# Attention and two dense layers on one core: a third score buffer, one score a round, v loaded in eight halves, w_in decoded in fixed rounds

## The chip, the core and the metric

The program runs on one core of a Trainium2 chip. The metric is the device time of one execution in microseconds. The kernel before takes 887.46 us in the median of three runs (885.88 to 888.39). The profile was taken of a further execution of 892.93 us.

## The reference

There are three layers one after the other. The first is attention with batch 4, 12 heads, 448 positions and 64 features a head, in which two 12x12 matrices mix the heads, one before the softmax and one after it:

```
scores = q k^T / 8                              # b h i j
scores = einsum('bhij,hg->bgij', scores, w_pre)
attn   = softmax over j of scores
attn   = einsum('bhij,hg->bgij', attn, w_post)
x      = attn @ v                               # then (b, s, 768)
```

The second layer computes `h = gelu(x @ w_in)` with 1024 columns, splits it in `u` and `v`, normalises `v`, mixes its positions with a 448x448 matrix, and returns `x + (u * v_s) @ w_out`. The third rotates `x` by angles `x @ w_theta`, mixes positions with two 448x448 matrices, and adds `relu(u @ w_ch)`. Inputs are float32; the dense weights come as 64-bit words that the kernel decodes into a high and a low part.

## The kernel before, in words

Attention works on tiles `(b, t)`: in each of 4 batches the 448 queries are cut into tiles of 120, 120, 120 and 88 (`TILES`). A *round* is the unit of the loop at the end of `attention` (`for r in range(-LR, NR + 7)`). It handles a pair of blocks of ten queries by twelve heads, 120 partitions a block. A 120-query tile has 6 rounds, the 88-query tile has 4 rounds of pairs and one of a single block of eight queries. So a batch has 23 rounds, and there are `NR` = 92. Batch 1 begins at round 23, batch 2 at 46, batch 3 at 69.

For a tile, `scores(b, t, c)` runs six times, once for each pair of heads c: 8 matmuls q k^T into PSUM tile `psA` (one buffer of two banks), and one ScalarE copy into the tile's SBUF buffer `s` (pool `a_s`, L225). When all six are there, `relayout` (L236) sends the rows of a block through a DMA from `s` into a buffer `blk`, so that heads and queries lie on partitions; it is issued four rounds before the block is used (`LR`). There are six `blk` buffers, for three rounds. Two rounds before use (`LQ`) `premix` multiplies by w_pre into `psB` (L244), `rowmax` takes the maximum on VectorE (L250), and `expo` the exponential on ScalarE (L258). Then `recip` (GpSimd, L264), `recip2` (VectorE, L269) and `weigh` (GpSimd, L280) scale w_post by the reciprocal sums. In its own round `postmix` multiplies by those weights into `psC` (L302, three buffers, two a round). `at_hi` (ScalarE, L325) and `at_lo` (VectorE, L331) split the result in two float16 parts. When a tile is finished `attn_v` multiplies by v (L354), one c a round in the rounds behind it, and `out_x` and `store_x` write it to the scratch tensor xT.

Within a round each engine gets its instructions in the order of the loop body: relayout of round r+4, the list `early`, postmix, recip2 and weigh of the next round, `at_hi`, `at_lo`, the lists `front` and `mid`, premix to recip of round r+2, the second `at_lo`, then the lists `work` and `late`. Which step stands in which round and list is written out by the `put` calls. Every load and store goes through one queue, that of SyncE (SPq), in program order. A DMA in this queue that has to wait holds up those behind it.

The places that the change touches:

- *Score buffers.* `a_s` has two buffers. The scores of a tile begin in the round behind the one in which the last relayout of the tile two before it is issued, and that tile's buffer is the one they write. The function `units` spreads the six scores of a tile over the rounds of the tile before. As an 88-query tile has five rounds, one round in each batch gets two scores (rounds 14, 37 and 60).
- *v.* For batches 1 to 3, `load_v` loads v in four pieces (rounds 8, 7, 5 and 4 before z, with z the round before the batch), 128 partitions x 768 columns each (the last one on 64). `v_max` (L154) takes maxima two rounds later on VectorE, `v_turn` and `v_spread` carry them across partitions with two small matmuls into a tile `psV` from pool psA, and `v_mul` (GpSimd, L188), `v_hi` (VectorE, L193) and `v_lo` (GpSimd, L197) split v in two float16 parts, one c a round over six rounds.
- *Decoding of w_in.* 18 jobs (`extra`) decode 128x256 blocks: a load into `draw` in early of round W-2, ScalarE and VectorE steps in rounds W to W+2 (`words`, `value`, `high`, `low`), among them the ScalarE copy into `dh` in round W+1 (L602), and in early of round W+4 a store of `dh` to the scratch tensor win_d (L618). Pool `a_dec` has one buffer of each, so the copy of a job into `dh` waits until the store of the job before has landed. `JR0` and `JR1` place the jobs evenly: W = 8, 12, 16, 20, 25, 29, 33, 37, 42, 46, 50, 55, 59, 63, 67, 72, 76, 80.

At the end of attention the pools on the right side of SBUF are closed and the dense layers' tiles take their place; the loads of x and of the decoded w_in are issued from round 88 on (`tail`).

Of the kernel before, what the change touches and what calls it, by code (L numbers as in the profile page):

```python
# [6 lines left out]
F32 = mybir.dt.float32  # L7
# [5 lines left out]
ALU = mybir.AluOpType  # L13
AX = mybir.AxisListType
PSUM = bass.MemoryType.PSUM

B, H, S, D = 4, 12, 448, 64
NP = H // 2
# [9 lines left out]
LR, LQ = 4, 2  # L28
QO = 3
WARM = 8  # L30
JR0, JR1 = 8, 7
EXP_BITS = 0x7F800000


def attention(tc, nc, io, xT, B, extra, tail):
# [8 lines left out]
    NR = len(pairs)  # L44
    tiles = [(b, t) for b in range(B) for t in range(len(TILES))]
    nt = len(tiles)
    first, last = {}, {}
# [4 lines left out]
    with ExitStack() as es:  # L52
        early_es = ExitStack()

        def pool(name, bufs, **kw):
            return es.enter_context(tc.tile_pool(name=name, bufs=bufs, reuse_waits="tile", **kw))

        def pool_r(name, bufs, **kw):
            return early_es.enter_context(tc.tile_pool(name=name, bufs=bufs, side="right", reuse_waits="tile", **kw))

        s_p = pool_r("a_s", 2)
        k_p = pool_r("a_k", NP + 3)
        q_p = pool_r("a_q", 3)
        vr_p = pool_r("a_vr", 1)
# [1 line left out]
        psA = pool_r("psA", 1, space=PSUM)  # L66
# [9 lines left out]
        psC = pool("psC", 3, space=PSUM)  # L76
# [17 lines left out]
        ps = psC.tile([128, 512], F32, tag="psC", name="warm_ps")  # L94
# [36 lines left out]
        raws, kt, qt = {}, {}, {}  # L131
# [12 lines left out]
        vraw = vr_p.tile([128, 4, NP, 128], F32, name="vraw")  # L144
        nc.gpsimd.memset(vraw[:64, 3], 0.0)

        def load_v(b, j):
            p = slice(0 if j < 3 else 64, 128)
            nc.sync.dma_start(out=vraw[p, j], in_=io["vN"][b, 128 * j:min(128 * j + 128, S)].rearrange("p (c d) -> p c d", d=128))

        def v_max(b, j):
            if j == 0:
                raws["vmx", b] = sm_p.tile([128, 4, NP], F32, tag="vmx", name="vmx", bufs=1)
            nc.vector.tensor_reduce(out=raws["vmx", b][:, j], in_=vraw[:, j], axis=AX.X, op=ALU.max,  # L154
                                    apply_absolute_value=True)

        def v_join(b):
# [3 lines left out]

        def v_turn(b):

            ps = raws["vps", b] = psA.tile([128, 2, 512], F32, tag="psA", name="psV")[:, 0]
            nc.tensor.matmul(ps[:NP, :128], raws.pop(("vmx", b)), ident, start=True, stop=True)

        def v_top(b):
# [4 lines left out]

        def v_spread(b):

            ps = raws["vps", b] = psA.tile([128, 2, 512], F32, tag="psA", name="psV")[:, 0]
            nc.tensor.matmul(ps[:, :NP], ones, raws.pop(("dg", b)), start=True, stop=True)

        def v_scale(b):
# [191 lines left out]
        early, front, mid, work, late = {}, {}, {}, {}, {}  # L370

        def put(d, r, fn, *a):
            d.setdefault(r, []).append((fn, a))

        def units(T):
            lo, hi = first[tiles[T - 1]] - LR, first[tiles[T]] - LR - 1
            return [lo + (c * (hi - lo + 1)) // NP for c in range(NP)]

        for T in range(1, nt):
            b, t = tiles[T]  # L380
            u = units(T)
            for c in range(NP):
                put(front if u[c] not in u[:c] else work, u[c], scores, b, t, c)
            if T > 1:
                put(early, u[0] - QO, load_q, b, t)
            if t == 0:
                for c, r in enumerate(units(T - 1)):
                    put(early, r, load_k, b, c)
        for b in range(B):
            f = first[b, 0]  # L390
            z = f - 1 if b else 3
            for j, d in enumerate((8, 7, 5, 4) if b else (5, 4, 3, 2)):
                put(early, z - d, load_v, b, j)
                put(late, z - d + 2 if b else min(z - d + 2, z - 1), v_max, b, j)
            put(late, z - 1, v_join, b)
            put(work, z, v_turn, b)
            put(late, z, v_top, b)
            put(work, z + 1, v_spread, b)
            put(late, z + 1, v_scale, b)
            for c in range(NP):  # L400
                put(mid, z + 2 + c, v_mul, b, c)
                put(late, z + 2 + c, v_hi, b, c)
                put(mid, z + 3 + c, v_lo, b, c)
        for T in range(nt):
            b, t = tiles[T]
            for c in range(NP):
                if T == nt - 1:
                    r = last[b, t] + 1 + c // 3
                else:
                    r = last[b, t] + (min(2 + c, 6) if T == 0 else min(1 + c, 5 if t == 2 else 6))  # L410
# [2 lines left out]
                    put(late, r, out_x, b, t, c // 3)  # L413
                    put(early, r + (2 if T < nt - 1 else 1), store_x, b, t, c // 3)

        for j, fn in enumerate(extra):
            r = JR0 + (NR - JR0 - JR1) * j // len(extra)
            put(early, r - 2, fn[0], dec)
            words, value, high, low = fn[1:5]
            for i in range(2):  # L420
                put((mid, late)[i], r, words, dec, i)
                put((mid, late)[i], r + 1, high, dec, i)
            put(late, r, value, dec)
            put(late, r + 1, low, dec, 0)
            put(mid, r + 2, low, dec, 1)
            put(early, r + 4, fn[5], dec)
# [788 lines left out]
def build(tc, nc, io, out):  # L1215
    with tc.manual_schedule(), ExitStack() as top:
        dram = top.enter_context(tc.tile_pool(name="scratch", bufs=1, space=bass.MemoryType.DRAM))
        xT = dram.tile([DM, B * S], F32, name="xT")
        x2T = dram.tile([DM, B * S], F32, name="x2T")
        d = Dense(tc, nc, io, xT, x2T, out)  # L1220
        d.scratch(dram)
        right, left1, left2 = ExitStack(), ExitStack(), ExitStack()
        tail, win_es, last_u, end = moe1(d, left1, right)
        th_es = moe2(d, left2, win_es, last_u, left1)
        for i in range(4):
            tail.setdefault(-2 + 2 * i, []).append(d.step)
        jobs = d.decode_all(io["w_in"], HF, DFF, d.win_d)
        jobs += d.decode_all(io["w_in"], 0, HF, d.win_d, 128 * KE)
        attention(tc, nc, io, xT, B, jobs, tail)
        while d.at < len(d.units):  # L1230
            d.step()
        th_es.close()
        right.close()
        left2.close()
# [74 lines left out]
```

## Time and profile before

| what | value |
|---|---|
| median of three runs | 887.46 us |
| profiled execution | 892.93 us |
| its span, first to last instruction | 891.2 us |
| TensorE busy, share of the span | 854.0 us, 96% |
| VectorE, ScalarE, GpSimd busy | 74%, 60%, 28% |
| attention, to the first dense matmuls | to about 376 us |
| granted TensorE clock, mean | 0.992 |

The profile's busy times are means over the whole span. The attention rounds end at about 362 us; from 376 us on TensorE works on the dense layers almost without a gap. A table of stretches counts the matmuls of one line in each, and since a round of a pair has 64 postmix matmuls (L302), the count gives the number of rounds in the stretch.

### The profile page before, as it was taken

How to read it: one execution, taken by the hardware profiler on the slowest of the kernel's cores; microseconds unless marked ns; L12 is line 12 of the kernel's file. 1: busy time of each engine (PE TensorE's matmuls, PEld its weight loads, DVE VectorE, ACT ScalarE, POOL GpSimd, SP SyncE). 2: the span in 40 equal slices, each digit the busy share in tenths (PEclk: the TensorE clock that was granted, in tenths of full speed). 3: DMA queues.
4: the chain of work that ended last, by engine and by line, in shares of the span. 5: the costliest groups of instructions: out<-in, count | busy, mean ns of one | idle time of the engine just before them, and what ended most of it. 6: DMA issues, size and time to landing. Idle time of an engine off the chain costs nothing.

```text
span 891.2 us, 29399 instructions
## 1 busy us (share of the span) xinstructions
PE 854.0 (96%) x12008; PEld 673.9 (76%) x12008; DVE 660.7 (74%) x1471; ACT 535.3 (60%) x1202; POOL 253.9 (28%) x453
## 2 busy tenths in 40 slices
PE   8899999999998999799999999998999999999998
PEld 2456556565665566589898989898989999999997
DVE  3887888788888888579999998969886358338221
ACT  5888789878897887466665767427535136016010
POOL 0272254225422642000000000016607228406421
PEclk9999999999999999899999999999999999999999
DMA  6567656675676545873385857997620311300301
GB/s 203 193 210 220 212 176 213 207 230 175 217 229 201 186 168 141 270 239 98 111 280 172 279 182 234 294 348 248 212 92 29 114 34 39 114 22 7 105 20 63
DMA packets 116343, 151.15 MB, mean 170 GB/s; under 512 B 26224, under 2 KB 100208, under 8 KB 116208
## 3 DMA queue, kind: packets, MB, share of 16 engines
q1 hardware_dynamic: 116208, 149.26, 52.8%
q8 instruction: 95, 1.56, 0.8%
q14 instruction: 40, 0.33, 0.1%
HBM read 78.38 MB, written 32.31 MB: 124 GB/s over the span
## 4 chain that ended last, share of the span: by engine, by line
PE 67%; DVE 9%; DMA 8%; ACT 6%; POOL 5%; issue 4%; SPq 1%; ACTq 0%; POOLq 0%; DVEq 0%
PE ps L554 46%; PE psC L302 6%; PE psB L244 5%; PE psA L219 4%; PE psD L354 4%; ACT e L258 2%; POOL vl L197 2%; ACT s L225 2%; DVE nmx L250 1%; DMA win_d<-dh 1%; POOL vraw L188 1%; DMA blk<-s 1%; POOL wr L280 1%; DMA xres<-xT 1%; ACT ah L325 1%
## 5 line engine op out<-in xcount | busy, mean ns | idle before, releaser
L258 ACT ACTIVATE e<-psB,nmx 128x448 f32<-128x448 f32 x180 | 113.1, 637 | 32.8 <-DVE nmx L250 31.6
L331 DVE SCALAR_TENSOR_TENSOR al<-psC,ah 128x480 f16<-128x480 f32 x180 | 116.3, 647 | 9.7 <-ACT ah L325 8.8
L250 DVE TENSOR_REDUCE nmx<-psB 128x1 f32<-128x448 f32 x180 | 103.9, 618 | 16.2 <-PE psB L244 13.9
L302 PE MATMUL psC<-wr,e 64*64 64x60 f32 x5632 | 106.4, 222 | 4.3 <-issue 1.9
L550 POOL TENSOR_TENSOR x2s<-x,x2s 128x384 fp32r<-128x384 f32 x28 | 28.8, 1049 | 284.8 <-ACT x2s L547 284.8
L244 PE MATMUL psB<-blk,kpre 64*64 64x448 f32 x720 | 104.0, 546 | 4.8 <-ACT e L258 3.9
L302 PEld LDWEIGHTS psC<-wr,e 64*64 64x64 f32 x5632 | 93.7, 135 | 17.0 <-POOL wr L280 7.5
L554 PE MATMUL ps<-wtok,z 128*128 128x448 f32 x504 | 104.8, 368 | 0.0
L219 PE MATMUL psA<-k,q 64*64 64x448 f32 (+2 forms) x768 | 96.5, 551 | 7.8 <-ACT s L225 5.6
L554 PEld LDWEIGHTS ps<-wtok,z 128*128 128x128 f32 x504 | 94.6, 188 | 9.5
L354 PEld LDWEIGHTS <-vh 128*64 128x64 f16 x1536 | 57.5, 112 | 58.0 <-issue 57.8
L325 ACT ACTIVATE ah<-psC 128x480 f16<-128x480 f32 x180 | 93.7, 581 | 10.3 <-PE psC L302 10.2
L554 PE MATMUL ps<-wth,x2s 128*128 128x384 f32 x504 | 93.0, 338 | 3.2 <-POOL x2s L550 2.1
L225 ACT ACTIVATE s<-psA 124x896 f32<-124x896 f32 (+1 forms) x90 | 84.2, 936 | 12.3 <-PE psA L219 7.6
L554 PEld LDWEIGHTS ps<-wth,x2s 128*128 128x128 f32 x504 | 87.1, 188 | 4.9 <-POOL x2s L550 3.0
L554 PE MATMUL ps<-u,wch 128*128 128x448 f32 x432 | 89.9, 368 | 0.0
L554 PEld LDWEIGHTS ps<-u,wch 128*128 128x128 f32 x432 | 81.1, 188 | 8.1
L550 POOL TENSOR_TENSOR z<-zz,z 128x384 fp32r<-128x384 f32 x56 | 64.4, 1170 | 55.7 <-ACT z L547 55.6
L244 PEld LDWEIGHTS psB<-blk,kpre 64*64 64x64 f32 x720 | 37.6, 132 | 50.0 <-ACT e L258 23.8
L547 ACT ACTIVATE u<-xres 128x448 fp32r<-128x448 f32 x24 | 13.8, 577 | 99.1 <-DVE xres L1123 99.1
L264 POOL TENSOR_SCALAR rc<-sum 128x2 f32<-128x2 f32 (+1 forms) x92 | 22.4, 244 | 176.1 <-ACT e L258 175.0
L280 POOL TENSOR_SCALAR wr<-w,rc 128x60 f32<-128x60 f32 x180 | 54.5, 317 | 53.3 <-DVE rc L269 43.0
(129 smaller groups left out, 1614.5 us busy)
## 6 DMA issues: line engine op xcount, KB each, us to landing
blk<-s SPq DMA_DIRECT2D x176, 210.0 KB
draw<-in_w_in SPq DMA_DIRECT2D x24, 256.0 KB
k<-in_kvT SPq DMA_DIRECT2D x24, 224.0 KB
xraw<-xT SPq DMA_DIRECT2D x24, 224.0 KB
xres<-xT SPq DMA_DIRECT2D x24, 224.0 KB
x2T<-xres SPq DMA_DIRECT2D x24, 224.0 KB
xres<-x2T SPq DMA_DIRECT2D x24, 224.0 KB
out<-uu SPq DMA_DIRECT2D x24, 224.0 KB
```

The source lines that it names most:

```text
L219: nc.tensor.matmul(ps[e][r, :S], q[p, o + r.start:o + r.stop], k[p], start=True, stop=True)
L225: nc.scalar.activation(out=out, in_=pair[:m, :, :S], func=AF.Copy, scale=0.125)
L244: nc.tensor.matmul(ps[e][c:c + 64, :S], kpre[k, e], blk[k], start=True, stop=True)
L250: nc.vector.tensor_reduce(out=nmx[r][:, e:e + 1], in_=ps[:, :S], axis=AX.X, op=ALU.max, negate=True)
L258: nc.scalar.activation(out=x, in_=ps[:, :S], func=AF.Exp, bias=m[:, e:e + 1], accum_out=sm[:, e:e + 1])
L280: nc.gpsimd.tensor_scalar(out=w, in0=wts[n], scalar1=rc[:, e:e + 1], scalar2=0.0, op0=ALU.mult, op1=ALU.add)
L302: nc.tensor.matmul(pc[r][h][c:c + 64, jc, :, SQ * e:SQ * e + SQ], x[p, c:c + 64], wr[r][e][p], start=(e == 0 and jc == 0), stop=(e == 1 an ...
L325: nc.scalar.activation(out=at_view(r, e, at[b, t][0]), in_=at_src(r, e), func=AF.Copy, scale=2.0 ** -17)
L331: nc.vector.scalar_tensor_tensor(out=al, in0=at_src(r, e), scalar=2.0 ** -17, in1=ah, op0=ALU.mult, op1=ALU.subtract)
L354: nc.tensor.matmul(ps[p, o:o + n], v[:, jc, p], a[:, i0:i0 + n], start=(o == 0 and m == 0), stop=(o > TI and m == len(terms) - 1))
L550: eng.tensor_tensor(out=out, in0=in_, in1=hi.bitcast(F32), op=ALU.subtract)
L554: self.nc.tensor.matmul(ps, l, r, start=(i == 0), stop=(i == len(terms) - 1))
```

## The change

`a_s` gets a third buffer, and the list `s_at` places one score in each round from -4 on, with two in rounds -3, 20 and 43. Next v of batches 1 to 3 is loaded in eight halves of 384 columns, one a round from z-11 to z-4, each with its own `v_max`; its splits are spread over eight rounds by `V_HI`. The tile `psV` comes from pool psC. K of the next batch is loaded five rounds before its score. The decode jobs stand at fixed rounds of each batch (`JOBS`), which gives W = 8, 12, 16, 20, 26, 32, 36, 40, 44, 49, 55, 59, 63, 67, 72, 76, 80, 84. Nothing that is computed changes.

```diff
-JR0, JR1 = 8, 7
+TWO_S = (-3, 20, 43)
+V_HI = (0, 1, 3, 4, 6, 7)
+JOBS = ((8, 12, 16, 20), (3, 9, 13, 17, 21), (3, 9, 13, 17, 21), (3, 7, 11, 15))
...
-        s_p = pool_r("a_s", 2)
+        s_p = pool_r("a_s", 3)
...
-        def load_v(b, j):
+        def load_v(b, j, c0=0, c1=NP):
             p = slice(0 if j < 3 else 64, 128)
-            nc.sync.dma_start(out=vraw[p, j], in_=io["vN"][b, 128 * j:min(128 * j + 128, S)].rearrange("p (c d) -> p c d", d=128))
+            src = io["vN"][b, 128 * j:min(128 * j + 128, S), 128 * c0:128 * c1]
+            nc.sync.dma_start(out=vraw[p, j, c0:c1], in_=src.rearrange("p (c d) -> p c d", d=128))
...
-            ps = raws["vps", b] = psA.tile([128, 2, 512], F32, tag="psA", name="psV")[:, 0]
+            ps = raws["vps", b] = psC.tile([128, 512], F32, tag="psC", name="psV")
...
+        s_at = sorted(list(range(-LR, NR)) + list(TWO_S))
         def units(T):
-            lo, hi = first[tiles[T - 1]] - LR, first[tiles[T]] - LR - 1
-            return [lo + (c * (hi - lo + 1)) // NP for c in range(NP)]
+            return s_at[NP * (T - 1):NP * T]
...
-                for c, r in enumerate(units(T - 1)):
-                    put(early, r, load_k, b, c)
+                for c in range(NP):
+                    put(early, u[c] - 5, load_k, b, c)
...
-            for j, d in enumerate((8, 7, 5, 4) if b else (5, 4, 3, 2)):
-                put(early, z - d, load_v, b, j)
-                put(late, z - d + 2 if b else min(z - d + 2, z - 1), v_max, b, j)
+            if b:
+                for i in range(8):
+                    a = b, i // 2, 3 * (i % 2), 3 * (i % 2) + 3
+                    put(early, z - 11 + i, load_v, *a)
+                    put(late, z - 9 + i, v_max, *a)
+            else:
+                for j, d in enumerate((5, 4, 3, 2)):
+                    put(early, z - d, load_v, b, j)
+                    put(late, min(z - d + 2, z - 1), v_max, b, j)
...
             for c in range(NP):
-                put(mid, z + 2 + c, v_mul, b, c)
-                put(late, z + 2 + c, v_hi, b, c)
-                put(mid, z + 3 + c, v_lo, b, c)
+                r = z + 2 + (V_HI[c] if b else c)
+                put(mid, r, v_mul, b, c)
+                put(late, r, v_hi, b, c)
+                put(mid, r + 1, v_lo, b, c)
...
-        for j, fn in enumerate(extra):
-            r = JR0 + (NR - JR0 - JR1) * j // len(extra)
+        at_rounds = [first[b, 0] + r for b in range(B) for r in JOBS[b]]
+        for r, fn in zip(at_rounds, extra):
```

SyncE's queue in rounds 39 to 41, before: `blk` are relayouts, `xT` is a store of finished attention, `draw` a load of w_in and `win_d` a store of it.

```order
L236 DMA blk_132<-s 120x1x448
L236 DMA blk_133<-s 120x1x448
L140 DMA q<-in_qT 128x724
L367 DMA xT<-x 128x3x120
L236 DMA blk_134<-s 120x1x448
L236 DMA blk_135<-s 120x1x448
L149 DMA vraw<-in_vN 128x768
L578 DMA draw<-in_w_in 128x512
L236 DMA blk_130<-s 96x1x448
L149 DMA vraw<-in_vN 64x768
L618 DMA win_d<-dh 128x2x256
```

The same queue in the same rounds of the changed kernel:

```order
L239 DMA blk_132<-s 120x1x448
L239 DMA blk_133<-s 120x1x448
L142 DMA q<-in_qT 128x724
L152 DMA vraw<-in_vN 128x384
L370 DMA xT<-x 128x3x120
L239 DMA blk_134<-s 120x1x448
L239 DMA blk_135<-s 120x1x448
L152 DMA vraw<-in_vN 64x384
L632 DMA win_d<-dh 128x2x256
L239 DMA blk_130<-s 96x1x448
L152 DMA vraw<-in_vN 64x384
```

The loads of v are half as large and begin three rounds earlier, and a store to win_d stands now in round 40, with the copy into `dh` that follows it in round 41 (before, stores stood in rounds 37 and 41).

GpSimd in two rounds of the splits of batch 1, before: `rc` and `wr` are the steps of every round, `vraw` is v_mul, `vl` is v_lo, `dh` the last step of a decode job.

```order
L197 TENSOR_TENSOR vl_2648<-vraw_145,vh_2647 128x512
L188 TENSOR_SCALAR vraw_145<-vraw_145,sv_2543 128x4x128
L264 TENSOR_SCALAR rc_2722<-sum_2717 128x2
L280 TENSOR_SCALAR wr_2794<-w5_128,rc_2722 128x60
L280 TENSOR_SCALAR wr_2796<-w5_128,rc_2722 128x60
L197 TENSOR_TENSOR vl_2750<-vraw_145,vh_2749 128x512
L188 TENSOR_SCALAR vraw_145<-vraw_145,sv_2543 128x4x128
L264 TENSOR_SCALAR rc_2825<-sum_2820 128x2
L280 TENSOR_SCALAR wr_2898<-w5_128,rc_2825 128x60
L280 TENSOR_SCALAR wr_2900<-w5_128,rc_2825 128x60
L197 TENSOR_TENSOR vl_2854<-vraw_145,vh_2853 128x512
```

GpSimd in the rounds of the second to fourth split of the changed kernel:

```order
L200 TENSOR_TENSOR vl_2759<-vraw_145,vh_2758 128x512
L267 TENSOR_SCALAR rc_2833<-sum_2828 128x2
L283 TENSOR_SCALAR wr_2904<-w5_128,rc_2833 128x60
L283 TENSOR_SCALAR wr_2906<-w5_128,rc_2833 128x60
L191 TENSOR_SCALAR vraw_145<-vraw_145,sv_2555 128x4x128
L267 TENSOR_SCALAR rc_2934<-sum_2929 128x2
L283 TENSOR_SCALAR wr_3003<-w5_128,rc_2934 128x60
L283 TENSOR_SCALAR wr_3005<-w5_128,rc_2934 128x60
L200 TENSOR_TENSOR vl_2962<-vraw_145,vh_2961 128x512
L191 TENSOR_SCALAR vraw_145<-vraw_145,sv_2555 128x4x128
L627 TENSOR_TENSOR dh_2918<-da_2814,dp_2816 128x256
```

Before, each of five rounds has both a v_lo and a v_mul; now three of nine rounds have both, three have v_mul alone and three v_lo alone.

## Rows read from the trace of the kernel before

**Rows 1.** The page, busy time of the engines over the span.

```profile
PE 854.0 (96%) x12008; PEld 673.9 (76%) x12008; DVE 660.7 (74%) x1471; ACT 535.3 (60%) x1202; POOL 253.9 (28%) x453
```

**Rows 2.** Stretches, line L302: us, matmuls, weight loads, granted clock, DMA share, GB/s.

```profile
73.90:95.00 21.10, 5.85 (x320) 5.18 (x320) 1.00 0.74 211
...
117.30:140.80 23.50, 7.29 (x384) 6.49 (x384) 1.00 0.49 164
140.80:161.00 20.20, 7.03 (x384) 6.22 (x384) 1.00 0.76 250
161.00:190.70 29.70, 9.13 (x448) 8.03 (x448) 0.94 0.71 204
...
250.90:275.60 24.70, 7.01 (x384) 6.21 (x384) 1.00 0.76 224
...
338.90:361.50 22.60, 8.36 (x448) 7.35 (x448) 1.00 0.51 131
```

**Rows 3.** The chain that ended last, one undisturbed round: start, us, what.

```profile
147.58 1.09 PE psC L302 x64
148.67 0.75 PE psA L219 x7
149.42 0.75 PE psB L244 x8
150.17 0.75 PE psD L354 x24
```

**Rows 4.** ScalarE's timeline in five places: start, us, instruction, idle before.

```profile
32.87 0.92 ACT L225 ACTIVATE s<-psA 124x896 f32<-124x896 f32 x1 [1.38 <-DMA blk<-s]
...
91.72 0.42 ACT L602 ACTIVATE dh<-da 128x256 fp32r<-128x256 f32 x1 [2.68 <-DVE vmx L154]
...
164.61 0.92 ACT L225 ACTIVATE s<-psA 124x896 f32<-124x896 f32 x1 [1.18 <-DMA blk<-s]
...
186.83 0.92 ACT L225 ACTIVATE s<-psA 124x896 f32<-124x896 f32 x1 [2.04 <-issue]
...
272.30 0.42 ACT L602 ACTIVATE dh<-da 128x256 fp32r<-128x256 f32 x1 [2.31 <-DMA win_d<-dh]
```

**Rows 5.** The chain, at two of these waits.

```profile
86.62 5.02 DMA win_d<-dh
...
158.81 5.70 DMA blk<-s
...
167.40 1.91 PE psC L302 x64
```

**Rows 6.** The chain, in the rounds of the v splits of batch 1.

```profile
124.01 0.60 POOL wr L280 x2
124.61 1.12 POOL vl L197
125.73 0.68 POOL vraw L188
...
126.44 0.43 DVE vh L193
...
127.78 0.60 POOL wr L280 x2
```

**Rows 7.** TensorE's and VectorE's timelines: a psV matmul, a second at_lo.

```profile
113.23 0.38 PE L176 MATMUL psV<-dg,ones 6*128 6x6 f32 x2 [0.44 <-ACT s L225]
...
151.30 0.65 DVE L331 SCALAR_TENSOR_TENSOR al<-psC,ah 128x480 f16<-128x480 f32 x1
```

**Rows 8.** SyncE's timeline, relayouts in a row: start, us of issuing, instruction.

```profile
12.42 5.33 SPq L236 DMA_DIRECT2D blk<-s  x6
...
345.29 3.25 SPq L236 DMA_DIRECT2D blk<-s  x2
```

**Rows 9.** The step to the dense layers: a stretch as in rows 2, the chain.

```profile
361.50:376.00 14.50, 1.16 (x64) 1.02 (x64) 0.86 0.98 336
...
363.12 7.34 DMA xraw<-xT
```

More of the change, by code (lines that the diff above doesn't have):

```diff
@@ L145, in attention, with v_max @@
         nc.gpsimd.memset(vraw[:64, 3], 0.0)
-        def load_v(b, j):
+        def load_v(b, j, c0=0, c1=NP):
             p = slice(0 if j < 3 else 64, 128)
-            nc.sync.dma_start(out=vraw[p, j], in_=io["vN"][b, 128 * j:min(128 * j + 128, S)].rearrange("p (c d) -> p c d", d=128))
-        def v_max(b, j):
-            if j == 0:
+            src = io["vN"][b, 128 * j:min(128 * j + 128, S), 128 * c0:128 * c1]
+            nc.sync.dma_start(out=vraw[p, j, c0:c1], in_=src.rearrange("p (c d) -> p c d", d=128))
+        def v_max(b, j, c0=0, c1=NP):
+            if j == 0 and c0 == 0:
                 raws["vmx", b] = sm_p.tile([128, 4, NP], F32, tag="vmx", name="vmx", bufs=1)
-            nc.vector.tensor_reduce(out=raws["vmx", b][:, j], in_=vraw[:, j], axis=AX.X, op=ALU.max,
+            nc.vector.tensor_reduce(out=raws["vmx", b][:, j, c0:c1], in_=vraw[:, j, c0:c1], axis=AX.X, op=ALU.max,
                                     apply_absolute_value=True)
@@ L173, in v_spread @@
         def v_spread(b):
-            ps = raws["vps", b] = psA.tile([128, 2, 512], F32, tag="psA", name="psV")[:, 0]
+            ps = raws["vps", b] = psC.tile([128, 512], F32, tag="psC", name="psV")
             nc.tensor.matmul(ps[:, :NP], ones, raws.pop(("dg", b)), start=True, stop=True)
@@ L381, in attention @@
             u = units(T)
+            assert u[-1] < first[tiles[T]] - LR
+            assert T < 3 or u[0] > last[tiles[T - 3]] - LR
             for c in range(NP):
@@ L414, in attention @@
                     put(early, r + (2 if T < nt - 1 else 1), store_x, b, t, c // 3)
-        for j, fn in enumerate(extra):
-            r = JR0 + (NR - JR0 - JR1) * j // len(extra)
+        at_rounds = [first[b, 0] + r for b in range(B) for r in JOBS[b]]
+        assert len(at_rounds) == len(extra)
+        for r, fn in zip(at_rounds, extra):
             put(early, r - 2, fn[0], dec)
```

## The prediction

> **What bounds the kernel now.** I read first the page's busy times. TensorE is busy for 96% of the span [rows 1], but matmul ends are modelled, so that alone doesn't say where it is late. Then I read the chain of waits in an undisturbed round: postmix 1.09, score 0.75, premix 0.75, one attn_v 0.75, in all 3.34 us with nothing between [rows 3]. That is TensorE's floor for a round with one score. Third came the table of stretches, cut where rounds begin, in which 64 postmix matmuls are a round. The six rounds 31 to 36 take 20.20 us against 6 x 3.34 = 20.04: no loss. Rounds 14 to 18 take 21.10 against 16.70, rounds 25 to 30 take 23.50 against 20.04, rounds 37 to 43 take 29.70 against 23.38, rounds 60 to 65 take 24.70 against 20.04; in three of these four, 0.75 is the second score of one round [rows 2, 3]. The last rounds, which have no score, take 22.60/7 = 3.23 each and have other limits. So the loss sits in known places of the attention part, and the dense part isn't touched. Fourth, ScalarE's waits say what ended last in those places. Three score copies wait, 1.38, 1.18 and 2.04; two copies into dh wait, 2.68 and 2.31 [rows 4]. The chain names the relayout behind the second of them (5.70 from issue to landing) and the win_d store behind the first dh (5.02) [rows 5]. The releaser "VectorE vmx" printed at the 2.68 is only what came last by the profile; the store's 86.62 + 5.02 = 91.64 fits the start at 91.72. The copy at 186.83 has no releaser in the row, but it is the first score of a tile, as the 164.61 is, and I take it for the same wait. Fifth, the v splits have a chain of their own on GpSimd and VectorE [rows 6].
>
> A word on DMA. Six relayouts of the first tile (120 queries, rows 12 partitions apart) are issued in 5.33 us, 0.89 each; two of an 88-query tile (8 apart), with little else in the queue (131 GB/s over the stretch), need 3.25, or 1.62 each [rows 2, 8]. So while an 88-query tile is relaid out (rounds 14 to 18, 37 to 41, 60 to 64), its two relayouts fill 3.25 of a round's 3.34, and any load or store comes on top. All the waits of rows 4 but the first lie in those rounds or just behind them.
>
> **The change part by part.**
>
> *Third score buffer.* It removes the wait for the tile before last: 1.38 + 1.18 + 2.04 = 4.60 [rows 4]. [...] (1 - 0.94) x 29.70 = 1.8 us is what the half clock cost at most; I take 1.5. Together 6.1 at most. What is late next: the 1.38 lies in the start-up, with nothing behind it, and is kept. The others lie where the queue is full. Rounds 37 to 41 hold before four pairs and a single relayout (4 x 3.25 + 1.62 = 14.6), and v 1,344, two stores 512, w_in 256, q 362 and xT 180 KB, which is 2,654 KB and 10.6 us at the best rate of rows 2 (250 GB/s): 25.2 us for rounds whose floor is 17.5. After, three of the eight halves of v (576 KB, 2.3 us) and one store (1.0 us) are elsewhere: 21.9 against 16.7. The queue is still 5 us too full; relayouts are asked for two rounds early and take part of that, the stores do not. The copy into dh follows its store by one round, in rounds 37 and 41 now, inside the full stretch. So I let the dh waits take back 3.7 of 6.1, a wait and a half like the 2.31 and 2.68. Net -2.4 us; bounds -6.1 (nothing comes back) and 0 (all of it).
>
> *One score a round.* The second score costs TensorE 0.75 and ScalarE 0.92 [rows 3, 4] in rounds 14, 37 and 60. After, one is in round -3, before the first block has landed, where TensorE waits anyway: nothing. Two are in rounds 20 and 43, which prepare a single block, so premix is half (0.38): 3.34 + 0.75 - 0.38 = 3.7. By floors this saves 0.75 once and twice half a premix, 1.5; as rounds 14, 37 and 60 are full of DMA work that has to be done in any case, I take -1.0, with bounds -3.0 (three times 0.75, and ScalarE's part) and 0.
>
> *Splits over eight rounds.* The chain in such a round is wr 0.60, vl 1.12, vraw 0.68, VectorE's vh 0.43 and some VectorE work between, from one wr to the next 127.78 - 124.01 = 3.77 [rows 6], 0.43 over the floor, in about four rounds of a batch, three batches: 5.2. After, rounds with both v_lo and v_mul stand alone, and the next round makes up for them, since weigh runs a round ahead. I leave 0.4 a batch: -4.0. Bounds -5.5 and -1.0. In batch 0 the splits stay as they are.
>
> *psV in psC.* Removed are two waits of psV for the score copy in each batch, 0.44 for the second [rows 7]. Added is one: psC has three buffers and a round takes two, so the postmix behind the second psV needs the second at_lo of the round just ended, which ends 151.30 + 0.65 = 151.95, 1.03 behind the start of the next postmix (147.58 + 3.34) [rows 3, 7]. psV's own 0.38 hides part: 0.65 are left. The first psV stands in the round of a single block, which takes one buffer, and adds no wait. Behind the waiting postmix stand the next score and premix. 0.44 and its like against 0.65: 0 for the sum, bounds -3 and +3 over four batches.
>
> *Fixed decode rounds.* Before, two stores made dh wait, 4.99 together [rows 4]. The pairs of rounds 16/17 and 63/64 remain. In the first a half of v (192 KB, 0.8 us) is now ahead of the store, in the second 96 instead of 384 KB. A store in round 59, behind a half of v, is new to the full stretch. +1.0; bounds -5.0 (none waits) and +6.0. Eight maxima of half the length for four cost VectorE nothing it hasn't to spare in a 3.34 us round; 12 more issues of half a microsecond on SyncE lie beside its waits for free blk buffers. Where these covers are gone they are in the bounds just given.
>
> *The end.* The last store of w_in moves from round 84 to 88, just ahead of the dense loads, in a stretch at 98% DMA share and 336 GB/s [rows 9]: 256 KB, 0.75 us. Against that, the memory that the first loads take no longer belongs to the last tile's score buffer. 0, bounds -1.0 and +0.8.
>
> [...]
>
> The sum: -2.4 - 1.0 - 4.0 + 0 + 1.0 + 0 = -6.4 us. On the profiled execution, 892.93 (span 891.2 and 1.7 around it), that gives 886.5. That execution is 5.5 over the median of the runs, and I carry the difference over to the median: 887.46 - 6.4 = 881.1, so 881.
>
> **The rivals.**
>
> *Slower: the stores.* Every pair of store and dh copy in and before the full stretches waits (rounds 16/17, 36/37, 40/41, 44/45, 59/60, 63/64), for 2.5 us as in rows 4 and 0.9 more for the half of v ahead of it: 6 x 3.4 = 20.4, less the 4.99 of before, +15.4. With -6.1 - 1.0 - 4.0 from the rest it is +4.3: 891.8. It decides where a store lands more than about 6.9 us after its round begins: a round of 3.34 and the 3.5 us at which dh comes in ScalarE's next. For it speaks that SyncE is in order and the halves stand ahead of the stores; against it, that every wait drains the queue for the next store.
>
> *All of it.* DMA has room once v comes evenly: -6.1 - 2.5 - 5.0 - 2.0 (dh waits and psV) = -15.6: 872. For it speaks 250 GB/s without loss in rounds 31 to 36 [rows 2]; against it the 1.62 us a relayout.
>
> *Nothing.* The full stretches need their time whatever waits in them: the buffer gives back all but the 1.4 of the start, the scores give 0, psV costs 1.5, the splits give 3.0, the stores cost 2.0: -0.9, 886.5.
>
> **How the numbers follow.** Chances: the forecast 0.48, all of it 0.20, nothing 0.20, slower 0.12. A difference under 0.3%, 2.7 us, can't be told from none. Faster by more: most of the forecast, all of the second, a little of the third: 0.67. Within: 0.20. Slower: 0.13. The forecast's own range is 877 to 885. For 8 in 10 it reaches to most of "all of it" below and into the third rival, short of the slower one, above: 873.5 to 889.5.
>
> **What would show it.** Right: no score copy on ScalarE waits over 0.5 us for a relayout; the rounds of the splits of batches 1 to 3 run at 3.3 to 3.5; dh waits of 2 to 4 us stand in rounds 17, 41 and 64; psV no longer waits for ScalarE, and the postmix behind the second psV waits about half a microsecond for an at_lo. Wrong: five or six dh waits (slower), none (all of it), a premix that waits for blk, or another stretch of half clock, above all in the step to the dense layers, where the mean is 0.86 now [rows 9] and a shift either way is worth some microseconds.

## The result, and the profile after

The changed kernel is slower: 895.90 us (median of 6 runs, 894.55 to 902.05) beside 888.21 for before, ratio 1.0086, interval [1.0058, 1.0114]. That is 7.7 us more; 6.4 less were forecast. The profiled execution of after took 894.55 (span 892.8).

The stretches again, TensorE's postmix line alone, with the rounds of [rows 2]: 14 to 18, 25 to 30, 31 to 36, 37 to 43, 60 to 65, 83 to 89, and the first 10 us of the step to the dense layers. Columns as there.

```profile
75.20:97.80 22.60, 6.05 (x320) 5.30 (x320) 0.93 0.67 186
121.80:143.10 21.30, 7.58 (x384) 6.50 (x384) 1.00 0.52 171
143.10:164.00 20.90, 7.17 (x384) 6.24 (x384) 1.00 0.78 250
164.00:196.20 32.20, 8.59 (x448) 7.47 (x448) 1.00 0.67 197
252.80:280.40 27.60, 8.03 (x384) 7.04 (x384) 0.91 0.66 192
341.90:366.00 24.10, 8.11 (x448) 7.17 (x448) 1.00 0.61 163
366.00:376.00 10.00, 1.38 (x64) 1.12 (x64) 1.00 1.05 353
```

The rounds of the splits (second row) are 2.2 us shorter. The rounds of the 88-query tiles are longer by 1.5, 2.5, 2.9 and 1.5 (first, fourth, fifth and sixth row), though 14 to 18 and 60 to 65 no longer hold a second score, and the DMA share in the first three of them is lower than before. Something waits there that is not bytes alone.

What TensorE waits for from 20 to 360 us, before (the groups that change), as line, releaser, us in total, times, longest:

```profile
PE psA L219 <- ACT s L225: 4.8, 6, 1.9
PE psB L244 <- ACT e L258: 3.2, 4, 1.7
PE psC L302 <- issue: 1.9, 2, 1.1
PE psV L176 <- ACT s L225: 1.8, 4, 0.4
...
PE psV L165 <- ACT s L225: 1.5, 4, 0.8
```

And after:

```profile
PE psC L305 <- issue: 6.7, 7, 1.7
PE psB L247 <- ACT e L261: 5.2, 4, 1.8
PE psC L305 <- DVE vm L183: 3.6, 4, 1.3
PE psB L247 <- DMA blk<-s: 2.5, 1, 2.5
PE psC L305 <- DVE al L334: 1.7, 2, 1.3
...
PE psA L222 <- ACT s L228: 0.8, 2, 0.6
```

The waits for score copies went, 4.8 to 0.8, and those of psV. In came a premix that waits for an exponential (5.2 for 3.2, and the 2.5 printed with a relayout are another, as shown below), and a postmix that waits for VectorE (5.3). The stalls inside a postmix that have no releaser ("issue") differ between two profiles of one kernel as much as between kernels (before 1.9 and 4.8, after 6.7 and 4.8), so I don't count them to the change.

The exponentials are late because ScalarE stands in front of dh, the buffer that the decode jobs store from. These are the copies that answer to [rows 4]; the three score copies of those rows have no wait any more:

```profile
93.09 0.42 ACT L616 ACTIVATE dh<-da 128x256 fp32r<-128x256 f32 x1 [4.39 <-DMA win_d<-dh]
...
169.13 0.42 ACT L616 ACTIVATE dh<-da 128x256 fp32r<-128x256 f32 x1 [1.94 <-DMA win_d<-dh]
...
187.99 0.42 ACT L616 ACTIVATE dh<-da 128x256 fp32r<-128x256 f32 x1 [2.08 <-DMA win_d<-dh]
...
276.47 0.42 ACT L616 ACTIVATE dh<-da 128x256 fp32r<-128x256 f32 x1 [2.84 <-DMA win_d<-dh]
...
352.98 0.42 ACT L616 ACTIVATE dh<-da 128x256 fp32r<-128x256 f32 x1 [2.42 <-DMA win_d<-dh]
```

Five waits, 13.7 us, for two of 5.0. They stand in rounds 17, 37, 41, 64 and 85. SyncE's queue shows why the first is so long (start, us of issuing):

```profile
86.42 1.71 SPq L152 DMA_DIRECT2D vraw<-in_vN  x1
88.23 0.53 SPq L370 DMA_DIRECT2D xT<-x  x1
88.86 0.42 SPq L632 DMA_DIRECT2D win_d<-dh  x1
89.38 1.69 SPq L239 DMA_DIRECT2D blk<-s  x2
91.12 1.19 SPq L152 DMA_DIRECT2D vraw<-in_vN  x1
92.40 1.34 SPq L239 DMA_DIRECT2D blk<-s  x1
```

The store belongs to round 16, which begins at 81.90 on TensorE. SyncE comes to it at 88.86, two rounds later, because it has no gap: from 82.28 on it issues the two relayouts of that round, then q, v and the store of xT, 6.3 us in all. What lengthens single issues (1.71 for the half of v here, 0.53 for a smaller one at 93.79) the profile doesn't show. The copy into dh comes right behind the store, in round 17. Behind the copy, on ScalarE, stands the exponential that the next premix waits for (timeline of all engines):

```profile
93.41 0.62 ACT L261 ACTIVATE e<-psB,nmx 128x448 f32<-128x448 f32 x1
...
94.17 0.19 PEld L247 LDWEIGHTS psB<-blk,kpre 64*64 64x64 f32 x2 [3.33 <-ACT e L261]
94.17 2.38 PE L247 MATMUL psB<-blk,kpre 64*64 64x448 f32 x8 [2.55 <-DMA blk<-s]
```

The weight load names the exponential, the matmul a relayout. The relayout issued at 92.40 can't be what it needs: this premix is that of round 18, whose blocks SyncE issued from 82.28 on, and the block issued at 92.40 is first read two rounds later. So it is the exponential, and through it dh. TensorE has stood for 2.55, and the premix takes 2.38 for 0.75, its later matmuls 1.00 each for 0.54: the half clock. The granted clock is 0.50 here from 94.8 to 98.0 us, and again from 255.1 to 258.4 and from 279 to 282, in the stretches that now show 0.93 and 0.91.

### The profile page after: what moved, and what is told of

Same layout as the page of the kernel before. It is cut to its first block, busy times and chain, and to the rows that moved or that the text cites. A ratio compares the mean times of both kernels' runs of the same rounds, so it can differ in the third digit from the quotient of the medians.

```text
span 892.8 us, 29400 instructions
## 1 busy us (share of the span) xinstructions
PE 848.6 (95%) x12008; PEld 672.9 (75%) x12008; DVE 659.9 (74%) x1483; ACT 535.2 (60%) x1202; POOL 251.9 (28%) x453
## 4 chain that ended last, share of the span: by engine, by line
PE 68%; DVE 10%; ACT 7%; DMA 7%; issue 3%; POOL 3%; SPq 2%; ACTq 0%; POOLq 0%; DVEq 0%
PE ps L568 45%; PE psC L305 6%; PE psB L247 6%; PE psA L222 5%; PE psD L357 4%; ACT e L261 3%; DVE nmx L253 2%; DMA x2T<-xres 2%; ACT s L228 2%; DVE al L334 2%; ACT ah L328 1%; POOL vl L200 1%; DMA wth<-wth_d 1%; DMA win_d<-dh 1%; DMA draw<-in_w_in 1%
## 5 line engine op out<-in xcount | busy, mean ns | idle before, releaser
L305 PE MATMUL psC<-wr,e 64*64 64x60 f32 x5632 | 108.9, 223 | 13.9 <-issue 7.7
L222 PE MATMUL psA<-k,q 64*64 64x448 f32 (+2 forms) x768 | 94.7, 549 | 3.4 <-ACT s L228 2.0
L267 POOL TENSOR_SCALAR rc<-sum 128x2 f32<-128x2 f32 (+1 forms) x92 | 21.2, 231 | 186.8 <-ACT e L261 186.2
L561 ACT ACTIVATE u<-xres 128x448 fp32r<-128x448 f32 x24 | 13.8, 577 | 99.2 <-DVE xres L1137 99.2
L357 PE MATMUL psD<-ah,vh 128*64 128x120 f16 (+1 forms) x768 | 65.9, 220 | 2.3 <-DVE x L365 2.3
```

Of the source, the lines that this page charges most:

```text
L222: nc.tensor.matmul(ps[e][r, :S], q[p, o + r.start:o + r.stop], k[p], start=True, stop=True)
L267: nc.gpsimd.tensor_scalar(out=rc[:, :m], in0=sm[:, :m], scalar1=1e-9, scalar2=2.0 ** -14, op0=ALU.add, op1=ALU.mult)
L305: nc.tensor.matmul(pc[r][h][c:c + 64, jc, :, SQ * e:SQ * e + SQ], x[p, c:c + 64], wr[r][e][p], start=(e == 0 and jc == 0), stop=(e == 1 an ...
L357: nc.tensor.matmul(ps[p, o:o + n], v[:, jc, p], a[:, i0:i0 + n], start=(o == 0 and m == 0), stop=(o > TI and m == len(terms) - 1))
```

## The experiments

Each ratio is to runs of before on the same chip; 0.1% is 0.9 us.

**Parts taken out of after.** Two buffers for dh:

```diff
-        self.raw_bufs, self.mid_bufs, self.out_bufs = 1, 1, 1
+        self.raw_bufs, self.mid_bufs, self.out_bufs = 1, 1, 2
```

> The kernel after, with two buffers for dh, so that a copy into dh waits for the store before last. In the profile of after five copies into dh wait for a win_d store, 4.39, 1.94, 2.08, 2.84 and 2.42 us, 13.7 in all, against 5.0 in two of before; the kernel is 7.7 us slower than before. Theory S (one dh buffer, and stores that come late in the full queue): without these waits the time falls by 8 to 12, to 884 to 888. Theory Q (the queue has too much work in the rounds of the 88-query tiles, whoever waits): premix or a score copy waits for a relayout in their place, 893 to 896. In between, 889 to 892, both have a part.

0.999 [0.9969, 1.001], 887.24 us: 8.5 us less than after. No wait for win_d is left among ScalarE's. From 60 to 360 us the profile lists only these above 0.6:

```profile
ACT e L261 <- DVE nmx L253: 26.9, 43, 2.5
ACT ah L328 <- PE psC L305: 12.3, 15, 1.2
ACT s L228 <- PE psA L222: 1.2, 4, 0.6
```

The decode rounds of before:

```diff
-        at_rounds = [first[b, 0] + r for b in range(B) for r in JOBS[b]]
+        at_rounds = [8 + (NR - 15) * j // len(extra) for j in range(len(extra))]
```

> The kernel after, with the decode jobs in the rounds of before (spread evenly over rounds 8 to 84). S, if the fixed rounds are what puts stores into full stretches: two or three dh waits, 5 to 8 us in all, 887 to 891. Q: the bytes are the same, 894 to 897. A third theory, V (the halves of v ahead of the stores make them late, in whatever round): dh waits of 10 us or more stay, 893 to 896.

1.0068 [1.0041, 1.0096]. The copies into dh still wait, four times, 10.9 us. V in four pieces:

```diff
-                for i in range(8):
-                    a = b, i // 2, 3 * (i % 2), 3 * (i % 2) + 3
-                    put(early, z - 11 + i, load_v, *a)
-                    put(late, z - 9 + i, v_max, *a)
+                for j, d in enumerate((8, 7, 5, 4)):
+                    put(early, z - d, load_v, b, j)
+                    put(late, z - d + 2, v_max, b, j)
```

> The kernel after, with v loaded in four pieces 8, 7, 5 and 4 rounds ahead, as before, and its maxima in four. V: the dh waits of rounds 17 and 41 shrink to 2.5 at most, that of round 64 stays, 889 to 892. S with the fixed rounds as the cause: the waits stay, or grow behind the larger pieces, 894 to 898.

1.0044 [1.002, 1.0068], dh waits 9.7. So neither the rounds (1.6 us) nor the halves (3.7) alone make the loss, and both intervals meet that of after; with either taken back, copies into the one buffer still wait some 10 us. psV in psA, in `v_turn` and in `v_spread`:

```diff
-            ps = raws["vps", b] = psC.tile([128, 512], F32, tag="psC", name="psV")
+            ps = raws["vps", b] = psA.tile([128, 2, 512], F32, tag="psA", name="psV")[:, 0]
```

> The kernel after, with psV in psA again, as before. If psV in psC costs what stands against it in my sum (0.65 a batch and what it removes), the time moves by less than 2 us either way: 894 to 898. If psC's three buffers are what the new loss hangs on (the postmix in rounds 21 to 23 and 44 to 46 waits for VectorE there), it falls by 3 to 6: 890 to 893. S and Q have no part in it; the dh waits stay 12 to 15 us.

1.0021 [0.9999, 1.0043]: 5.8 us less, far more than I gave psV, with dh waits of 18.4 in its profile.

**Controls.** After and before once more, unchanged:

> The kernel after once more, unchanged, beside the same runs of before as the next three, for a second profile of it. All theories: a ratio of 1.007 to 1.010 to before. The profile tells which waits of the first are the kernel's own: the five dh waits (13.7 us) come back within a microsecond each by S; TensorE's stalls of 1.6 us inside a postmix, which no row names a releaser for, come at other places if they are chance.

> The kernel before once more, for a second profile: the first one was 4.7 us above the median of its runs. If that was the half clock in the step to the dense layers (10 us of it), this profile has less of it and the dense part starts 3 to 5 us earlier; if it was in the attention rounds, they end earlier.

1.0084 [1.0055, 1.0113] and 0.9992 [0.9967, 1.0016]. The dh waits of after come back, not within a microsecond but larger, the sixth one in round 60, 18.9 us in all:

```profile
ACT dh L616 <- DMA win_d<-dh: 18.9, 6, 5.1
```

The second profile of before took 891.85, again above the median of its runs (887.2 to 889.7 over seven sets). So two profiles of before against two of after show less of the loss than the timed runs do, and the sizes below are taken from ratios. Before with two dh buffers (the edit of the first run):

> The kernel before with two buffers for dh. S: the two waits of 2.68 and 2.31 (and one of 0.53) go, 3 to 5 us less than before: ratio 0.994 to 0.997. Q: score copies wait longer instead, ratio 0.999 to 1.001. If this gains as much as it does in the kernel after (8.6 us), the fixed rounds and the halves of v cost nothing through dh and S is wrong about where the loss came from.

0.9984 [0.9959, 1.0009]. The second dh buffer is worth 1.4 us there, less than the 3 to 5 I expected and not clear of nothing, and 8.5 in after: the change made the one buffer dear.

**psV.** Two dh buffers, and psV in psA (the two edits above); then psV in psA in the first batch alone:

> The kernel after with two buffers for dh and psV in psA. If psV in psC costs some 5 us of its own, as the run with psV in psA alone says (ratio 1.002 for 1.0086), the two gains add: ratio 0.992 to 0.995. If that run gained by what the waits for stores happened to hide, or by the step to the dense layers, no more than the run with two dh buffers: 0.998 to 1.000.

> The kernel after with two buffers for dh, and psV in psA in the first batch alone, in psC in the other three. In eight profiles the first exponential of round 8 starts 29.1 to 30.3 us after that of round 0 where psV is in psA, and 30.9 to 32.9 where it is in psC. If psV costs in the start-up above all, this run has most of the gain of the one with psV in psA throughout (ratio 0.9931, against 0.999 with two dh buffers alone): 0.994 to 0.997, and the start-up takes 29 to 30 us. If the later batches pay (a postmix that waits 0.77 for VectorE after each psV), it stays at 0.998 to 1.000.

0.9931 [0.99, 0.9962] and 0.9962 [0.9945, 0.9979], against 0.999 with psV in psC throughout. The two gains add, and about half of psV's price lies in the start-up, as far as the intervals tell. There after has these two waits, in the profile's timeline of TensorE, for which the run with the first batch in psA has none:

```profile
37.50 1.09 PE L305 MATMUL psC<-wr,e 64*64 64x60 f32 x59 [1.33 <-DVE al L334]
...
42.07 1.09 PE L305 MATMUL psC<-wr,e 64*64 64x60 f32 x59 [1.35 <-DVE vm L183]
```

In each later batch there is one:

```profile
118.71 1.09 PE L305 MATMUL psC<-wr,e 64*64 64x60 f32 x59 [0.77 <-DVE vm L183]
```

**Parts alone on before.** Third buffer, `s_at` and the loads of k, and nothing else of the diff; the same with two dh buffers; the splits (`V_HI`) alone:

```diff
-        s_p = pool_r("a_s", 2)
+        s_p = pool_r("a_s", 3)
...
-            lo, hi = first[tiles[T - 1]] - LR, first[tiles[T]] - LR - 1
-            return [lo + (c * (hi - lo + 1)) // NP for c in range(NP)]
+            return s_at[NP * (T - 1):NP * T]
```

> The kernel before with the third score buffer and one score a round alone (psV, the splits, v and the decode rounds as before; k is loaded five rounds ahead of its score). My terms: -2.4 and -1.0, so a ratio of 0.996, with the score copies' waits gone and the two dh waits as they were or a little longer. Theory Q: what the buffer gives the dh waits take back, 0.999 to 1.001. If all of it comes (-6.1 and -2.5): 0.990 to 0.992.

> The kernel before with the third score buffer, one score a round, and two buffers for dh. If the one dh buffer alone takes the gain of the scores back (1.0019 without the second, 4.76, 1.65 and 1.90 us of dh waits in its profile), this has my -3.4 on top of what two dh buffers give before (0.9984): 0.993 to 0.996. If the full queue takes it back in any case: 0.997 to 1.000.

> The kernel before with the splits of batches 1 to 3 over eight rounds alone. My term: -4.0, ratio 0.9955, and the rounds of the splits at 3.2 to 3.6. If the time that the splits gave up is taken by the full queue or by the step to the dense layers: 0.998 to 1.000.

Scores: 1.0019 [0.9999, 1.0038], and 0.9999 [0.9977, 1.002] with two dh buffers: no gain in either. In the first, copies into dh wait 9.1 us for 5.0 and 5.6 in the two profiles of before, and rounds 14 to 18, which were to gain, take 22.9 for 21.1:

```profile
72.90:95.80 22.90, 5.85 (x320) 5.19 (x320) 0.94 0.70 201
```

Splits: 0.9987 [0.9973, 1.0001], though their rounds 25 to 30 take 20.7 for 23.5:

```profile
118.90:139.60 20.70, 7.01 (x384) 6.21 (x384) 1.00 0.55 185
```

Scores, splits and two dh buffers together, with psV, v and the decode rounds as in before:

```diff
-                put(mid, z + 2 + c, v_mul, b, c)
+                r = z + 2 + (V_HI[c] if b else c)
+                put(mid, r, v_mul, b, c)
...
-        self.raw_bufs, self.mid_bufs, self.out_bufs = 1, 1, 1
+        self.raw_bufs, self.mid_bufs, self.out_bufs = 1, 1, 2
```

> The kernel before with three parts: third score buffer and one score a round, the splits over eight rounds, and two buffers for dh; without the other parts of the change (psV in psC, v in eight halves, fixed decode rounds). If the fixed rounds and the halves of v give nothing of their own, this is as good as the kernel after with two dh buffers and psV in psA (ratio 0.9931): 0.992 to 0.995. If they do help once dh has two buffers, it is slower than that by 2 us or more: 0.995 to 0.998. If they still cost: 0.989 to 0.991.

0.9961 [0.9944, 0.9978], beside 0.9931 with the halves and fixed rounds: these help by about 2.7 us once dh has two buffers, or nothing (the intervals meet). Beside 0.9999 for scores and two dh buffers without the splits, these take 3.4 us here, for 1.2 alone.

**Towards a faster one**, from two dh buffers and psV in psA. V earlier, and then with it the last batch's jobs (the second part of the edit):

```diff
-                    put(early, z - 11 + i, load_v, *a)
-                    put(late, z - 9 + i, v_max, *a)
+                    r = z - (11 if i % 2 else 14) + i // 2
+                    put(early, r, load_v, *a)
+                    put(late, r + 2, v_max, *a)
...
-JOBS = ((8, 12, 16, 20), (3, 9, 13, 17, 21), (3, 9, 13, 17, 21), (3, 7, 11, 15))
+JOBS = ((8, 12, 16, 20), (3, 9, 13, 17, 21), (3, 9, 13, 17, 21), (3, 6, 9, 12))
```

> The kernel after with two buffers for dh and psV in psA, and the halves of v three to four rounds earlier (pairs 0 to 2 in rounds 14 to 11 ahead of the turn, pairs 3 to 5 in 11 to 8 ahead), so that one of eight is left in the rounds in which the 88-query tile is relaid out, for four. If bytes in those rounds are what still costs there: ratio 0.987 to 0.991 (0.9931 without), and rounds 18 to 24 and 41 to 47 take 22 to 23 us for 23.9 and 24.8. If the relayouts alone fill the queue, or the bytes are as dear three rounds earlier: 0.992 to 0.995.

> The same with the last batch's decode jobs in its rounds 3, 6, 9, 12 instead of 3, 7, 11, 15, so that the last store is asked for in round 85 and not 88, ahead of the last relayouts and not between them and the first load of the dense layers. In the profile with two dh buffers and psV in psA that load is issued 5.3 us behind the last relayout, in before 3.3. If the dense part begins when SyncE comes to its loads: 1.5 to 2 us less than the run without, 0.985 to 0.990. If it begins when the memory of the attention part comes free: no difference.

1.0028 [1.0007, 1.005] and 0.9989 [0.9968, 1.0011]. Here some halves were asked for ahead of the last splits of batch 0, which then used the new values, so that the two kernels compute something else: TensorE stood for splits on GpSimd that waited for loads (5.8 us from 20 to 90 us in the profile of the first), and the two times say nothing of the bytes. A round later for all (10 and 13 for 11 and 14), and then the jobs alone:

> The kernel after with two buffers for dh, psV in psA, the halves of v two to three rounds earlier (pairs 0 to 2 in rounds 13 to 10 ahead of the turn, pairs 3 to 5 in 10 to 7 ahead), and the last batch's decode jobs in its rounds 3, 6, 9, 12. If both are worth what the profiles of the two runs before it show behind batch 0 (1 to 2 us from 18 to 24 and 41 to 47, 1.5 to 3 at the step to the dense layers): ratio 0.986 to 0.990. If v's bytes are as dear earlier: 0.989 to 0.992, the same as the next run.

> The kernel after with two buffers for dh, psV in psA, and only the last batch's decode jobs in its rounds 3, 6, 9, 12. If the dense part begins when SyncE comes to its loads: 1.5 to 3 us less than without (0.9931): 0.989 to 0.992, and the first load of the dense layers follows the last relayout by 2 to 3 us for 5.3. If not: 0.992 to 0.995.

0.9949 [0.9931, 0.9967] and **0.9914 [0.9896, 0.9932]**, 880.13 us, the fastest. V some rounds earlier is no cheaper, if anything dearer. The last jobs are worth 1.5 us, within the intervals; their place in SyncE's queue is clear. After:

```profile
352.89 3.93 SPq L239 DMA_DIRECT2D blk<-s  x3
357.88 0.59 SPq L370 DMA_DIRECT2D xT<-x  x1
358.58 2.07 SPq L632 DMA_DIRECT2D win_d<-dh  x1
360.70 1.12 SPq L751 DMA_DIRECT2D xraw<-xT  x1
```

With the jobs earlier:

```profile
339.91 2.49 SPq L239 DMA_DIRECT2D blk<-s  x3
343.09 1.12 SPq L370 DMA_DIRECT2D xT<-x  x1
344.26 1.96 SPq L751 DMA_DIRECT2D xraw<-xT  x1
```

The first dense load follows the end of the last relayout's issue by 3.9 us there, by 1.9 here (1.7 in before); it is 3.9 too in the run with two dh buffers and psV in psA, from which this one differs by the jobs alone. Last, this fastest kernel with scores and k as in before (the edit of the scores alone, undone):

> The fastest version so far (the kernel after with two buffers for dh, psV in psA and the last decode jobs earlier, 0.9914) with two score buffers and the scores and k in the rounds of before. If the scores gain what I forecast once stores no longer wait: slower by 3 to 6 us, 0.995 to 0.998. If the queue takes their gain back here too: 0.990 to 0.993. If third buffer and single scores cost here, by keeping the queue further behind: under 0.989.

0.994 [0.9918, 0.9962], 2.3 us more. The score part has a gain of its own at best here, and below my 3.4; the intervals still meet.

## Why the prediction was wrong

Two steps were far off: psV, put at 0, cost some 5 us, and the score part, put at a gain of 7.1 before what dh takes back, gave none by itself. The waits for dh were right in kind and too small.

**Third buffer, -2.4.** The waits did go. The 1.5 for the half clock behind one of them no run shows by itself: in before the granted clock is 0.50 from 167.1 to 170.5 us, 3.4 us, and over rounds 37 to 43 of after its mean is 1.00, in the second profile 0.95. But the step said that dh takes back 3.7 of 6.1, and it took all: alone, the score part gives +1.7 us, with an interval from nothing to 3.4. With two dh buffers copies no longer wait, and still nothing is won (0.9999 against 0.9984). So dh is not all that takes the gain back. The profiles show that the time moves on to the rounds behind. In before, the first exponentials of rounds 14, 19 and 25 are 21.2 and 21.5 us apart (23.2 and 21.5 in its second profile); with two dh buffers 19.0 and 24.3, and with the score part too 19.3 and 24.6. From 37 to 44 that part takes two dh buffers from 29.0 to 27.2, and from 44 to 50 it brings them from 22.4 to 24.0; the latter stretch takes 23.5 us or more in all fifteen profiles with the score part and 22.4 or less in the five without. Of this 0.75 is the second score now in round 43. That a SyncE queue which the score waits had let catch up holds up the rest is argued, not shown.

**The waits for dh, 3.7 and +1.0: right in kind, too small.** With the 4.99 of before the sum allowed 9.7 us; 13.7 and 18.9 came. I expected them in rounds 17, 41 and 64; 37 and 85 wait too, in the second profile also 60. In time they cost 7.1 (8.5 less the 1.4 that before pays as well) for 4.7. The fixed rounds as such are near their +1.0: taken back, they give 1.6, not clear of nothing. The rival with the stores had the mechanism, and its condition held: a landing over 6.9 us into the round (93.00 - 81.90 = 11.1 for round 16). Its 20.4 us of waits were too many. It still came out at 891.8 and not 896, because it had psV and the end at 0 and kept 11.1 us of gains, of which 6.2 came (below).

**psV, 0 with bounds of 3: the largest miss of a single term.** 5.2 us with two dh buffers (0.999 to 0.9931), 5.8 with one. In a later batch the size was close (0.77 for 0.65), but the step named the wrong release: the postmix waits for VectorE to read psV (vm), not for an at_lo. And it left out batch 0, where first scores and each postmix take psC too (2.7). The listed waits don't make up the price: 5.3 in after for 3.3 of psV's own in before. Where the other 3 us arise isn't shown.

**Splits, -4.0.** Right where they stand, 2.2 us in batch 1 alone; timed alone -1.2, beside the score part and two dh buffers -3.4. So their gain comes once other waits are out of the way; each of these has some 2 us of doubt.

**One score a round, -1.0,** is not separated from the buffer; together they are +1.7 and not -3.4. Its floors were added up wrongly too: rounds 20 and 43 have half a premix before as well, so they give one second score, 0.75, and not 1.5.

**The end, 0.** Some 1.5 us lost, within the intervals: the store of round 88 takes 2.07 us of SyncE's time ahead of the dense loads. I counted its bytes (0.75) and not that.

On the sum: 7.1 for dh, 5.2 for psV and 1.5 for the end make 13.8. Without them the parts that were to gain are worth 0.9914 against 0.9984 for before with two dh buffers, 6.2 us. That 13.8 - 6.2 gives the 7.6 measured is no check: the four are steps of one chain of ratios and have to add up. Against the forecast, dh is 2.4 dearer, psV 5.2, the end 1.5, and the gains are 6.2 for 11.1 (6.1, 1.0 and 4.0): 14.0, the whole miss, each with 2 to 4 us of doubt. The 6.2 hold the halves of v and the fixed rounds too; scores and splits by themselves give 2.0 (0.9961 against 0.9984).

## What to carry to other kernels

Before a wait is removed beside a full in-order queue, look for the next single-buffered tile that the queue frees: here the wait moved there, and doubling that tile (2 KB a partition) took back 8.5 us. Even so the gain need not come: look at the rounds behind, too, for where the time goes. Price a store not by its bytes but by when the queue comes to it, and see what stands behind the engine that waits. When a tile changes its pool, walk through every place in which that pool is full, the start-up too.

## What the runs showed of the hardware

One relayout is far dearer than I took it for (1.62). The last block of an 88-query tile reads eight partitions in a row (104 to 111). In after it lands 2.97, 2.18, 3.25 and 2.77 us behind the DMA ahead of it, in the four batches. While it is alone the core moves 49 GB/s (stretch with all engines; share and GB/s last):

```profile
95.60:97.60 2.00, 2.00 (x30) 1.12 (x24) 1.30 (x3) 1.13 (x3) 1.06 (x3) 0.50 0.48 49
```

172 KB at 49 GB/s are 3.5 us, an estimate. A 120-query relayout (210 KB, ten source partitions 12 apart) lands 0.8 to 1.1 us behind the DMA ahead of it (those issued from 192.0 to 194.9 us in after). The block is issued behind the stores that come late (at 92.40, the store at 88.86), so it doesn't explain these. What makes it slower than the larger one, no run shows; what it costs the loads behind it, and whether a layout that sets its rows further apart helps, wasn't tried.
